# Causal attention and a two-stage mixer on one core: first loads four rows to a partition, scores in two jobs, a fourth Strassen pair and new ranks

## The chip, the core and the metric

The kernel runs on one core of a Trainium2 chip. The metric is the device time of one execution in microseconds; lower is better. The kernel before takes 565.9 us (median of 3 runs, 565.84 to 566.09).

## What is computed

```python
# q, k, v: (4, 12, 448, 64); seq 448, d_model 12 * 64 = 768
scores = scale * np.matmul(q, k.transpose(0, 1, 3, 2))
scores = np.where(np.triu(ones, k=1), -1e9, scores)          # causal
attn = np.exp(scores - scores.max(-1, keepdims=True))
attn = attn / (attn.sum(-1, keepdims=True) + 1e-09)
x = heads side by side of np.matmul(attn, v)                 # (4, 448, 768)
# the mixer; weights arrive as float64
h = np.maximum(x.T @ w_tok1, 0.0) @ w_tok2                   # 448 -> 256 -> 448, per batch
u = x + h.T
h2 = np.maximum(u @ w_ch1, 0.0) @ w_ch2                      # 768 -> 1536 -> 768
out = u + h2
```

## The kernel before, in words

**Jobs and a planner.** The kernel doesn't write its instructions in program order. It makes jobs (`Plan.job`), each with the engines that may do it and a cost in nanoseconds for each, the jobs that it needs, the buffers and PSUM banks that it holds, and a rank. `Plan.emit` then plays a clock of its own over those costs: whenever an engine is free it gives it the ready job of lowest rank, and writes that job's instructions. The order of instructions on each engine is therefore fixed when the program is built; on the chip each engine works through its own list in order and waits on semaphores. The costs and the ranks decide the order and nothing else.

**Fillers.** Up to 75 us on the planner's clock, TensorE (PE) is given matmuls of no use (`keep_warm`, L602, 128x512 bf16 on the mask) whenever it has no ready job and has been busy for less than a share `KEEP` of the time just past. They stand in PE's list like any other matmul.

**Attention.** The 48 heads are 24 pairs, in order of batch. `load_pair` fetches a pair's keys and queries (SP's queue; the queries of pair 0 on ACT's) in four DMAs each (L635), cut so that every partition gets 14 runs of 32 numbers, and `prep` turns them with one VectorE (DVE) 32x32 block transpose each (L667). `heads` makes the causal scores in 14 matmuls (L695) on four 64x64 corners of PE, fourteen blocks of 64 queries, into four PSUM banks; DVE adds the mask and takes the row minimum of the negated scores (L712), ScalarE (ACT) takes the exponential with its sum (L724), GpSimd (POOL) or another engine adds the guard (L743), DVE takes the reciprocal (L746), and the blocks are normalised (L343 on ACT, L345 on POOL or DVE). The probabilities are turned on PE (`flip`, L781) for pairs 0 to 11 and by DMA transpose for the others. `values` (L882) multiplies with v on 128x64 halves of PE, and `xturn` (L928) turns the result for the token stage.

**Mixer.** All products are in float32 split into a high and a low part, three matmuls for one. `tokens` (L974, L1007) runs three times per batch. `channels` (L1056) runs by `STAGES`: an entry (quarter of the 12 hidden blocks, batches) does `NF` = 3 hidden blocks (18 matmuls each and batch), then six output tiles with 9 matmuls each and batch, each added to `u` by DVE (L1124). For batches 2 and 3 some hidden blocks are done instead by `group`: a pair of hidden blocks times two batches is a 2x2 product of blocks, and Strassen's form needs 7 products of 9 matmuls (L1376) instead of 8. The output side of a group (L1444) has 6 matmuls per tile, and one DVE add. `combined` makes the sums of the weights, `mixtures` those of the inputs; before, `mixtures` runs late, rebuilds batch 2's input from its two parts (`again`) and keeps the sums in buffers that attention has left.

```python
STAGES = ((0, (0,)), (1, (0, 1)), (2, (0, 1)), (3, (0, 1)), (0, (1, 2)), (3, (2, 3)), (0, (3,)))
GROUPS = ((3, 4), (5, 6), (7, 8))
```

The last stage ends in `finish`, which adds, turns (L1472) and sends the last tile of the output.

Of the kernel before, what the change touches and what calls it, by code (L numbers as in the profile page):

```python
# [19 lines left out]

class Slot:


    def __init__(self, ring):
        self.ring = ring
        self.index = ring.uses
        self.left = 0
        self.tile = None
        ring.uses += 1

    def take(self):
        self.ring.taken.append(self)
# [16 lines left out]
class Bank:  # L49


    def __init__(self, plan, kind, share):
        self.plan, self.kind, self.share = plan, kind, share
        self.left = 0
        self.bank = None

# [4 lines left out]
    def take(self):  # L61
        p = self.plan
        self.bank = p.banks.pop(0)
        p.used[self.kind] = p.used.get(self.kind, 0) + 1
# [6 lines left out]
class Job:  # L71
    def __init__(self, order, costs, fn, rank, moved, lock=False):
        self.order, self.costs, self.fn, self.rank, self.moved, self.lock = order, costs, fn, rank, moved, lock
        self.waits = 0
        self.ready = 0.0
        self.after = []
        self.takes = []
        self.holds = []
# [4 lines left out]
class Plan:  # L83
# [7 lines left out]
    WINDOW, KEEP, WARM = 3400.0, 0.65, 75000.0  # L91
    LAG = {"pe": 230.0, "act": 150.0, "dve": 150.0, "pool": 150.0, "sp": 100.0}
    OWN = {"pe": 0.0, "act": 100.0, "dve": 130.0, "pool": 100.0, "sp": 100.0}
# [28 lines left out]
    def job(self, costs, fn, needs=(), holds=(), rank=0.0, moved=0.0, lock=False):  # L122

        j = Job(len(self.jobs), costs, fn, rank, moved, lock)
# [4 lines left out]
        for s in holds:  # L129
            if s.left == 0:  # L130
                j.takes.append(s)
            s.left += 1
# [4 lines left out]
    def emit(self):  # L137
        now = 0.0
        free = dict.fromkeys(self.ENGINES, 0.0)
        port = {"dve": 0.0, "pool": 0.0}  # L140
        dma = 0.0

        def until(j, e, t):
# [3 lines left out]
            return t + j.costs[e]  # L147
# [17 lines left out]
        while left:  # L165
# [3 lines left out]
            for e in self.ENGINES:  # L169
# [4 lines left out]
                while ready[e]:  # L174
# [4 lines left out]
                    open_ = all(s.open() for s in j.takes) and self.fits(j)  # L179
# [29 lines left out]
                end = until(pick, e, now)  # L209
                if e == "pool" or (e == "dve" and pick.lock):  # L210
                    port[e] = end
                free[e] = end
                if e == "pe":
                    self.spans.append((now, end))
                if pick.moved:
                    dma = end = max(end + 650.0, dma) + pick.moved
                    end += 800.0
                heapq.heappush(events, (end, 0, pick.order, pick))
# [25 lines left out]
def kernel(  # L244
# [72 lines left out]
    def act_ps(n):  # L317
        return 160.0 + 0.833 * n

    def act_sb(n):  # L320
        return 200.0 + 0.833 * n

    def dve1(n):
        return 150.0 + 1.04 * n
# [1232 lines left out]
```

## Time and profile before

| | |
|---|---|
| median of 3 runs | 565.9 us (565.84 to 566.09) |
| the profiled execution | 566.33 us, its span 564.6 us |
| busy PE / DVE / ACT / POOL | 548.2 / 395.0 / 304.7 / 223.1 us |
| PE matmul records | 3512, of them 55 fillers |

The page gives the engines' busy times; the windows give the same by stretch; the chain of waits follows the work that ended last back through what released it; the timeline lists an engine's instructions with the idle time ahead of each in brackets. A busy PE in the windows and the page is one with a matmul in flight. A float32 matmul on a part of the array has two records.

### The profile page before, as it was taken

Reading aid. Unit: us, or ns where it says so; the run is one execution under the profiler, and the core shown is the slowest. Engines: PE = TensorE matmul, PEld = TensorE weight load, DVE = VectorE, ACT = ScalarE, POOL = GpSimd, SP = SyncE. Lnnn points to the kernel's source line nnn. Section 1 sums busy time; section 2 is a strip of 40 time slices with the busy share of each in tenths; the row PEclk is TensorE's granted clock in tenths of the full one; section 3 lists DMA queues with packets and bytes.
Section 4 is the critical chain, followed back from the end, with each engine's and each line's share of the span. In section 5 each row is a group of like instructions: output and inputs, shape, how many; then the busy total and the mean of one; then the engine's idle time right before and its main releaser. Section 6 shows DMA issues by size and latency. Waiting matters only on the chain.

```text
span 564.6 us, 10295 instructions
## 1 busy us (share of the span) xinstructions
PE 548.2 (97%) x3512; PEld 473.5 (84%) x3512; DVE 395.0 (70%) x925; ACT 304.7 (54%) x746; POOL 223.1 (40%) x320
## 2 busy tenths in 40 slices
PE   8789999999999999999999999999999999999996
PEld 4467888878888988988988988988999998999995
DVE  4575868588777677778867687566576668677835
ACT  3678888787687566776667754674143120111010
POOL 2465675535352321430353621353356546232001
PEclk9999999999999999999999999999999999999999
DMA  6777647576988689789996766766221030312525
GB/s 112 157 154 149 155 104 174 161 180 150 197 224 190 149 203 204 177 222 200 217 217 132 151 111 122 148 126 127 62 74 56 29 111 2 111 55 86 126 57 99
DMA packets 230340, 77.37 MB, mean 137 GB/s; under 512 B 206544, under 2 KB 219024, under 8 KB 230288
## 3 DMA queue, kind: packets, MB, share of 16 engines
q1 hardware_dynamic: 217056, 74.99, 58.6%
q10 hardware_dynamic: 13232, 1.72, 1.8%
q8 instruction: 28, 0.46, 0.3%
q14 instruction: 24, 0.20, 0.1%
HBM read 49.15 MB, written 14.94 MB: 114 GB/s over the span
## 4 chain that ended last, share of the span: by engine, by line
PE 90%; SPq 3%; ACT 3%; DMA 2%; DVE 1%; issue 0%; POOL 0%; DVEq 0%; ACTq 0%
PE ps L1056 48%; PE ps L1444 8%; PE ps L882 7%; PE ps L1376 6%; PE ps L1007 5%; PE ps L974 5%; PE ps L695 5%; PE ps L781 3%; SPq L635 2%; PE ps L928 2%; DMA wl<-in_moe_w_tok_dram 1%; ACT prob L724 1%; SPq L400 1%; ACT pt L343 0%; DMA kq<-in_q_dram 0%
## 5 line engine op out<-in xcount | busy, mean ns | idle before, releaser
L1124 DVE TENSOR_TENSOR u<-ps,u 128x448 f32<-128x448 f32 x107 | 66.3, 622 | 47.1 <-PE ps L1056 33.6
L724 ACT ACTIVATE prob<-prob,stat 128x448 f32<-128x448 f32 (+6 forms) x168 | 84.0, 504 | 26.1 <-DVE stat L712 25.9
L345 POOL TENSOR_SCALAR prob<-prob,stat 128x448 f32<-128x448 f32 (+6 forms) x125 | 69.9, 572 | 39.7 <-DVE stat L746 36.7
L1056 PE MATMUL ps<-gh,wh 128*128 128x448 f32 x216 | 80.6, 373 | 0.0
L1056 PE MATMUL ps<-gh,wl 128*128 128x448 f32 x216 | 79.0, 366 | 0.0
L1056 PE MATMUL ps<-gl,wh 128*128 128x448 f32 x216 | 79.0, 366 | 0.0
L1056 PE MATMUL ps<-uh,wh 128*128 128x448 f32 x198 | 75.0, 379 | 0.0
L1056 PE MATMUL ps<-uh,wl 128*128 128x448 f32 x198 | 72.5, 366 | 0.0
L1056 PE MATMUL ps<-ul,wh 128*128 128x448 f32 x198 | 72.4, 366 | 0.0
L345 POOL TENSOR_SCALAR wh<-wf 128x768 fp32r<-128x768 f32 x27 | 23.1, 854 | 113.4 <-PE ps L1056 65.1
L712 DVE CUSTOM_DVE_ANT_0 prob<-ps,mask 128x448 f32<-128x448 f32 (+6 forms) x168 | 62.3, 412 | 0.3 <-PE ps L695 0.3
L743 POOL TENSOR_SCALAR stat<-stat 128x3 f32<-128x3 f32 (+1 forms) x43 | 13.3, 309 | 96.5 <-ACT prob L724 95.0
L882 PE MATMUL ps<-pt,vraw 128*64 128x448 f32 (+3 forms) x384 | 46.8, 386 | 1.4 <-ACT pt L343 1.4
L882 PEld LDWEIGHTS ps<-pt,vraw 128*64 128x64 f32 x384 | 25.4, 136 | 25.0 <-issue 14.0
L349 ACT COPY pt<-pt 128x512 uint16<-128x512 uint16 (+1 forms) x46 | 36.8, 875 | 15.5 <-DMA pt<-prob 15.4
L1056 PEld LDWEIGHTS ps<-gh,wh 128*128 128x128 f32 x216 | 40.6, 188 | 3.7
L1056 PEld LDWEIGHTS ps<-gl,wh 128*128 128x128 f32 x216 | 40.6, 188 | 3.5 <-DVE gl L1092 0.3
L1056 PEld LDWEIGHTS ps<-gh,wl 128*128 128x128 f32 x216 | 40.5, 188 | 3.2
L695 PEld LDWEIGHTS ps<-kq,kq 64*64 64x64 f32 x672 | 36.0, 132 | 8.3 <-issue 4.2
L695 PE MATMUL ps<-kq,kq 64*64 64x448 f32 (+6 forms) x672 | 41.8, 383 | 0.0
L354 DVE TENSOR_TENSOR wl<-wf,wh 128x768 fp32r<-128x768 f32 x35 | 35.9, 1033 | 8.5 <-ACT wh L343 4.9
L1056 PEld LDWEIGHTS ps<-uh,wh 128*128 128x128 f32 x198 | 37.2, 188 | 3.7
(144 smaller groups left out, 1224.2 us busy)
## 6 DMA issues: line engine op xcount, KB each, us to landing
wraw<-in_moe_w_ch_dram SPq DMA_DIRECT2D x24, 768.0 KB, 5.3
wf<-scratch SPq DMA_DIRECT2D x30, 384.0 KB, 3.2
scratch<-wf SPq DMA_DIRECT2D x24, 384.0 KB, 5.8
vraw<-in_v_dram SPq DMA_DIRECT2D x48, 96.0 KB, 2.4
out_dram<-kq SPq DMA_DIRECT2D x68, 56.0 KB, 1.8
kq<-in_k_dram SPq DMA_DIRECT2D x60, 56.0 KB, 3.9
kq<-in_q_dram SPq DMA_DIRECT2D x56, 56.0 KB, 2.5
gh<-in_k_dram SPq DMA_DIRECT2D x36, 56.0 KB, 2.3
```

What stands on the lines that cost most here:

```text
L345: eng[e].tensor_scalar(dst, src, scale, 0.0, op0=ALU.mult, op1=ALU.add)
L349: nc.scalar.copy(out, in_)
L354: eng[e].tensor_tensor(dst, a, b, op=ALU.subtract)
L695: nc.tensor.matmul(scores[r].tile[lanes, WHERE[c]:WHERE[c] + wide(c)], lhsT=qe.tile[LANES[j], c * QC:(c + 1) * QC], rhs=ke.tile[LANES[j], ...
L712: nc.vector.tensor_tensor_reduce(out=part(c, r), in0=ps.tile[:, WHERE[c]:WHERE[c] + wide(c)], in1=mask[:, S - wide(c):], scale=-SCALE, sca ...
L724: nc.scalar.activation(part(c, r), part(c, r), AF.Exp, bias=stat.tile[:, 0, AT[c]:AT[c] + 1], scale=-1.0, accum_out=stat.tile[:, 1, AT[c]: ...
L882: nc.tensor.matmul(ps.tile[LANES[j], c * QC:(c + nq) * QC], lhsT=s.tile[:, kb, j], rhs=view[:, o:o + nq, j], start=(kb == 0), stop=(n == 3),)
L974: nc.tensor.matmul(ps.tile[:, :PART], lhsT=w[:, c, m * P:(m + 1) * P], rhs=x.tile[:, c, :], start=(n == 0), stop=(n == len(work) - 1),)
L1056: nc.tensor.matmul(ps.tile[:, :S], lhsT=x.tile[:, at_:at_ + P], rhs=y, start=(n == 0 and i == 0), stop=(n + 1 == w[2] and i == 2),)
L1124: eng[e].tensor_tensor(u, ps.tile[:, :S], u, op=ALU.add)
L1376: nc.tensor.matmul(ps.tile[:, :S], lhsT=l()[:, t * P:(t + 1) * P], rhs=r, start=(t == 0 and n == 0), stop=(t == half - 1 and n == 2),)
L1444: nc.tensor.matmul(ps.tile[:, :S], lhsT=l.tile[:, t * P:(t + 1) * P], rhs=r.tile, start=(n == 0), stop=(n == 3 * len(fs) - 1),)
```

## The change

It does six things:

1. The keys and queries of pairs 0 and 1 are loaded with four neighbouring rows to a partition (112 partitions, two DMAs each instead of four; runs of 256 bytes in the tile instead of 128) into the buffers `uh` and `ul`, turned by four PE transposes each (`turn_runs`, L768 after the change) and copied back from PSUM by ACT or DVE. DVE's block transposes of these four tensors go.
2. The scores of a pair are two jobs: rounds 0 and 1, then rounds 2 and 3, each with its own two PSUM banks. The order of the 14 matmuls alternates between the two heads.
3. Hidden blocks 9 to 11 of batches 2 and 3 leave `channels` and become a group of one block (11), which is plain, and a fourth Strassen pair (9, 10).
4. `mixtures` is written right after attention, takes the inputs from `u` before anything is added to it (`again` goes), keeps some sums in the token weights' buffers, and adds to `u` wait for it.
5. `store` turns its tiles into the buffers `h1h` and `h1l`.
6. The planner has other costs, lags, and models of the DMA rings and of PE's change between tile shapes; KEEP is 0.7; a table `NUDGE` of some 110 numbers moves ranks of single jobs.

```diff
+NUDGE = {
+    "load_pair.load": {2.5: -0.3, 4.5: 1, 6.5: 4, 32.5: -38, 44.5: 24},
...
-    WINDOW, KEEP, WARM = 3400.0, 0.65, 75000.0
+    WINDOW, KEEP, WARM = 3400.0, 0.7, 75000.0
...
-    STAGES = ((0, (0,)), (1, (0, 1)), (2, (0, 1)), (3, (0, 1)), (0, (1, 2)), (3, (2, 3)), (0, (3,)))
+    STAGES = ((0, (0,)), (1, (0, 1)), (2, (0, 1)), (3, (0, 1)), (0, (1, 2)), (0, (3,)))
...
-    GROUPS = ((3, 4), (5, 6), (7, 8))
+    GROUPS = ((11,), (9, 10), (3, 4), (5, 6), (7, 8))
...
+            def whole(e, s=s, src=src):
+                make(s, [RUNS, RUN, 2, D], F32)
+                for j in range(2):
+                    eng[e].dma_start(
+                        out=s.tile[:, :, j], in_=src[b, 2 * t + j].rearrange("(p c) d -> p c d", c=RUN)
+                    )
...
+    def turn_runs(s, x, js, rank):
+
+        ps = share("t")
+
+        def turn(e):
+            bank(ps)
+            for c in range(RUN):
+                nc.tensor.transpose(
+                    ps.tile[:, c * RUNS:(c + 1) * RUNS], flat(s.tile[:, c]), ident[:RUNS, :RUNS]
+                )
+
+        def back(e):
+            copy(
+                e, make(x, [P, S], F32).rearrange("p (t c) -> p t c", c=RUN),
+                ps.tile[:, :S].rearrange("p (c t) -> p t c", c=RUN),
+            )
+
+        a = plan.job({"pe": pe(0, 0, 0, 0)}, turn, js, [s, ps], rank, turn=True)
+        return plan.job({"act": act_ps(S), "dve": dve1(S)}, back, [a], [ps, x], WRANK)
...
-        m = plan.job({"pe": 1900.0}, qk, ready + [last_qk[0]], holds, rank)
-        last_qk[0] = m
+        for rg, cost in zip(RG, (930.0, 740.0)):
+            holds = [x for r in rg for x in (scores[r], probs[r])] + [ke, qe, stat]
+            m = plan.job({"pe": cost}, lambda e, rg=rg: qk(e, rg), ready + [last_qk[0]], holds, rank, tiled=True)
...
-            x1, j1, f1 = mix("T1", t, p1, at(u3, t), ALU.subtract, [i1] + n3, [e1, u3])
+            x1, j1, f1 = mix("T1", t, at(u2, t), at(u3, t), ALU.subtract, [n2, n3], [u2, u3])
...
-    for stage in range(len(STAGES) - 2):
+    mixtures()
+    for stage in range(len(STAGES) - 1):
         channels(stage)
-    mixtures()
-    channels(len(STAGES) - 2)
-    for number in range(len(GROUPS)):
-        group(number, 6.0 + number * 0.63)
+    at = FIRST_GROUP
+    for number, fs in enumerate(GROUPS):
+        group(number, at)
+        at += SPAN[len(fs) - 1]
```

SP's list at its head, before (kq, gh, gl hold a pair's raw keys or queries, vraw its values; x4 is four DMAs):

```order
L635 DMA kq_106<-in_k_dram 32x14x32 x4
L635 DMA gh_126<-in_k_dram 32x14x32 x4
L635 DMA gl_134<-in_q_dram 32x14x32 x4
L644 DMA vraw_98<-in_v_dram 128x3x64 x2
L648 DMA vraw_98<-in_v_dram 64x2x64
L635 DMA gh_176<-in_k_dram 32x14x32 x4
L635 DMA gl_186<-in_q_dram 32x14x32 x4
L644 DMA vraw_100<-in_v_dram 128x3x64 x2
L648 DMA vraw_100<-in_v_dram 64x2x64
```

The same place of SP's list now:

```order
L707 DMA uh_109<-in_k_dram 112x4x64 x2
L707 DMA uh_117<-in_k_dram 112x4x64 x2
L707 DMA ul_126<-in_q_dram 112x4x64 x2
L724 DMA vraw_98<-in_v_dram 128x3x64 x2
L728 DMA vraw_98<-in_v_dram 64x2x64
L724 DMA vraw_100<-in_v_dram 128x3x64 x2
L728 DMA vraw_100<-in_v_dram 64x2x64
L715 DMA gh_172<-in_k_dram 32x14x32 x4
L715 DMA gl_198<-in_q_dram 32x14x32 x4
```

Six issues are gone ahead of pair 1's queries' end, and the values of pair 1 have moved ahead of pair 2's keys and queries.

DVE's list at its head, before (the four transposes are pairs 0 and 1; the ISA rows are L712 of pair 0 with the read of its minimum):

```order
L596 MEMSET zero 128x64
L667 STREAM_TRANSPOSE kq_142<-kq_106 128x448
L667 STREAM_TRANSPOSE kq_150<-kq_111 128x448
L667 STREAM_TRANSPOSE kq_174<-gh_126 128x448
L667 STREAM_TRANSPOSE kq_181<-gl_134 128x448
L712 ISA prob_0_90,stat_184<-ps_156,mask 128x448
L712 ISA stat_184 128x1
L712 ISA prob_0_91,stat_184<-ps_157,mask 128x384
```

DVE's list at its head now:

```order
L665 MEMSET zero 128x64
L826 ISA prob_0_90,stat_187<-ps_162,mask 128x448
L826 ISA stat_187 128x1
L826 ISA prob_0_91,stat_187<-ps_163,mask 128x384
L826 ISA stat_187 128x1
L826 ISA prob_0_91,stat_187<-ps_163,mask 128x128
```

No transpose stands ahead of pair 0's masking any more. Further down, pair 0's reciprocal stood behind the transpose of pair 2's keys and now stands ahead of it.

PE's list at the scores of pair 2, before (L695; `ps` are PSUM banks; the first six of 14):

```order
L695 MATMUL ps_309<-kq_216,kq_247 64x448
L695 MATMUL ps_310<-kq_216,kq_247 64x384
L695 MATMUL ps_311<-kq_216,kq_247 64x320
L695 MATMUL ps_312<-kq_216,kq_247 64x256
L695 MATMUL ps_310<-kq_216,kq_247 64x128
L695 MATMUL ps_312<-kq_216,kq_247 64x192
```

The same place of PE's list now (L806 scores, L895 turning of probabilities, L671 a filler):

```order
L806 MATMUL ps_295<-kq_240,kq_270 64x448 x2
L806 MATMUL ps_296<-kq_240,kq_270 64x384 x2
L806 MATMUL ps_296<-kq_240,kq_270 64x128 x2
L895 MATMUL ps_305<-ident,prob_0_93 128x128 x4
L671 LDWEIGHTS mask
L671 MATMUL ps_89<-mask 128x512
L806 MATMUL ps_322<-kq_240,kq_270 64x256 x2
L806 MATMUL ps_321<-kq_240,kq_270 64x320 x2
```

Before, the 14 matmuls of a pair always stood together; now other work stands between the halves of some pairs.

## Rows read from the trace of the kernel before

**Rows 1.** The page, busy us, share of the span, instructions:
```profile
PE 548.2 (97%) x3512; PEld 473.5 (84%) x3512; DVE 395.0 (70%) x925; ACT 304.7 (54%) x746; POOL 223.1 (40%) x320
```

**Rows 2.** Windows: stretch, its length, each engine's busy us, PE's granted clock, DMA share:
```profile
0.00:20.00 20.00, 15.65 (x116) 8.81 (x120) 8.77 (x37) 8.90 (x25) 7.07 (x29) 1.00 0.69 137
20.00:45.00 25.00, 19.74 (x189) 14.24 (x182) 17.23 (x60) 18.29 (x61) 14.04 (x29) 1.00 0.74 142
45.00:65.00 20.00, 20.00 (x182) 15.72 (x183) 14.55 (x59) 18.12 (x62) 13.02 (x25) 1.00 0.71 146
65.00:160.00 95.00, 93.96 (x751) 80.19 (x750) 70.94 (x196) 76.31 (x214) 48.54 (x77) 1.00 0.69 168
160.00:440.00 280.00, 280.00 (x1706) 246.20 (x1705) 201.09 (x451) 167.30 (x364) 102.73 (x132) 1.00 0.69 152
440.00:520.00 80.00, 78.61 (x388) 72.36 (x387) 55.25 (x82) 10.67 (x17) 33.21 (x28) 1.00 0.21 65
```

**Rows 3.** Chain of waits, in order of time: start us, us, what:
```profile
22.45 2.23 DMA gl<-in_q_dram
...
44.97 1.95 PE ps L882 x16
...
51.73 1.08 PE ps L602 x5
...
58.26 0.44 PE ps L928 x4
```

**Rows 4.** Timeline of PE, start: start us, us, engine, line, operation [idle before <-releaser]:
```profile
1.40 5.75 PE L602 MATMUL ps<-mask 128*128 128x512 bf16 x17 [1.40 <-POOL mask L364]
7.08 1.74 PE L695 MATMUL ps<-kq,kq 64*64 64x448 f32 x28
8.76 2.76 PE L602 MATMUL ps<-mask 128*128 128x512 bf16 x12
...
62.83 0.38 PE L974 MATMUL ps<-xh,w1hi 128*128 128x256 f32 x1
```

**Rows 5.** Timeline of PE's weight loads: two of the first fillers' loads:
```profile
4.78 0.15 PEld L602 LDWEIGHTS <-mask 128*128 128x128 bf16 x1 [0.28 <-issue]
5.21 1.45 PEld L602 LDWEIGHTS <-mask 128*128 128x128 bf16 x7 [0.28 <-issue]
```

**Rows 6.** Timeline of DVE, pairs 0 to 2:
```profile
5.10 1.17 DVE L667 STREAM_TRANSPOSE kq<-kq 128x448 f32<-128x448 f32 x2 [4.18 <-DMA kq<-in_k_dram]
...
9.07 0.65 DVE L667 STREAM_TRANSPOSE kq<-gl 128x448 f32<-128x448 f32 x1 [1.77 <-DMA gl<-in_q_dram]
9.64 0.59 DVE L712 CUSTOM_DVE_ANT_0 prob<-ps,mask 128x448 f32<-128x448 f32 x1
...
13.10 0.65 DVE L667 STREAM_TRANSPOSE kq<-gh 128x448 f32<-128x448 f32 x1 [1.00 <-DMA gh<-in_k_dram]
```

**Rows 7.** Timeline of ACT: the first exponential of pair 0:
```profile
10.28 0.67 ACT L724 ACTIVATE prob<-prob,stat 128x448 f32<-128x448 f32 x1 [6.20 <-DVE stat L712]
```

**Rows 8.** Timeline of SP's queue, DMA issues:
```profile
5.07 2.05 SPq L635 DMA_DIRECT2D gl<-in_q_dram  x4
```

**Rows 9.** DMA issues of the page: times, KB each, us to landing:
```profile
vraw<-in_v_dram SPq DMA_DIRECT2D x48, 96.0 KB, 2.4
```

**Rows 10.** Chain of waits, two stretches of PE alone:
```profile
439.81 13.41 PE ps L1056 x66
453.21 10.96 PE ps L1376 x54
```

**Rows 11.** Timeline of PE around one pair's scores:
```profile
58.97 0.38 PE L602 MATMUL ps<-mask 128*128 128x512 bf16 x1
59.27 1.74 PE L695 MATMUL ps<-kq,kq 64*64 64x448 f32 x28
```

**Rows 12.** The page's groups: DVE's adds to u:
```profile
L1124 DVE TENSOR_TENSOR u<-ps,u 128x448 f32<-128x448 f32 x107 | 66.3, 622 | 47.1 <-PE ps L1056 33.6
```

**Rows 13.** Timeline of PE: the first output of the first Strassen pair that waits:
```profile
467.57 0.47 PE L1444 MATMUL ps<-gl,wh 128*128 128x448 f32 x1 [1.39 <-DVE gl L1312]
```

More of the change, by code (lines that the diff above doesn't have):

```diff
@@ L18 @@
 PSUM = bass.MemoryType.PSUM
+NUDGE = {
+    "token_weights.<lambda>": {3.5: -11},
+    "xturn.<lambda>": {-1: -18, 37: 12},
+    "load_pair.load": {2.5: -0.3, 4.5: 1, 6.5: 4, 32.5: -38, 44.5: 24},
+    "heads.low": {2: 10, 6: 1},
+    "xturn.twice": {1: 9, 9: 6, 13: 11},
+    "load_pair.blocks": {2: 0.3, 6: -1, 10: -12, 12: -8, 36: -4, 38: 28, 40: 27},
+    "by_tensor.evac": {4: -3},
+    "values.pv": {4: 2, 12: 6, 24: -12},
+    "values.evac": {4: 24},
+    "heads.recip": {6: 3, 20: 5, 44: 1},
+    "tokens.tok1": {8.5: -32, 32.5: -5},
+    "by_tensor.flip": {8: -3.2, 18: 2},
+    "split_u.hi": {12.5: -1.5},
+    "prep.turn": {10.5: -7, 42.5: -5},
+    "heads.expo": {12: -1.1, 18: 6, 22: 0.1, 24: 0.04, 38: 42, 42: -2},
+    "xturn.lo": {11: 24, 19: 10, 33: 6, 37: 12},
+    "by_tensor.norm": {14: -4, 16: 14},
+    "heads.guard": {16: 12, 42: 34},
+    "heads.<lambda>": {20: -2, 34: -13, 42: -31, 44: -24, 46: 18},
+    "tokens.tok2": {24.5: -3, 28.5: 4},
+    "by_dma.split": {26: -2, 40: 15},
+    "xturn.turn": {31: 5},
+    "by_dma.turn": {34: -3, 42: 18},
+    "by_dma.norm": {42: -0.2},
+    "channel_weights.<lambda>": {12: -10, 19: -6},
+    "channels.up": {28.667: 4, 29.333: 10, 39.667: 7, 40.167: 5, 40.833: 14, 45.333: 14, 47.333: 16},
+    "channels.down": {30: -18, 30.5: -5, 37.75: -22, 38.5: 17, 44: -13, 54.25: 5, 55: 31.6, 55.5: 31.3, 77.09: -32},
+    "add.plus": {-6: 16},
+    "narrow.load": {16: -5, 23: -15, 26: -6, 33: -3},
+    "narrow.join": {17: 16},
+    "narrow.size": {30: 21},
+    "group.up": {57.34: 3, 57.68: 6},
+    "hidden.lo": {-6: 7},
+    "group.down": {60.23: 4, 69.75: 1.6},
+    "group.product.do": {59.85: 6, 60.39: 10, 60.66: 7, 63.36: -11, 66.87: 4, 67.68: 9, 68.22: 35},
+    "combined.split.lo": {-4.93: 10},
+    "parts.<lambda>": {-4.93: 2},
+}
 class Slot:
@@ L131, in job @@
                 j.takes.append(s)
+            elif s not in j.takes:
+                j.joins.append(s)
             s.left += 1
@@ L178, in emit @@
                         continue
-                    open_ = all(s.open() for s in j.takes) and self.fits(j)
+                    open_ = all(s.got for s in j.joins) and all(s.open() for s in j.takes) and self.fits(j)
                     if open_ and len(j.costs) > 1:
@@ L383, with narrow @@
     CRANK, CSTEP, CLEAD, WLEAD, TRANK = 2.0 * H - 6.0, 6.0, -9.0, 6.0, 3.5
-    def narrow(n, shape, source, f, rank, needs=(), raw=None):
+    def narrow(n, shape, source, f, rank, needs=(), raw=None, issues=1):
         raw = raw or slot("wraw")
@@ L415, in join @@
             )
-        j = plan.job({"sp": 520.0}, load, holds=[raw], rank=rank, moved=move(shape[0] * n * 8))
-        j = plan.job({"act": act_sb(n)}, size, [j, *needs], [raw, f], rank)
+        moved, ring = (3000.0, 60) if n > 2 * P else (800.0, 16)
+        j = plan.job({"sp": 530.0 * issues}, load, holds=[raw], rank=rank, moved=moved, ring=ring)
+        j = plan.job({"act": 115.0 + 0.92 * n}, size, [j, *needs], [raw, f], rank)
         j = plan.job({"dve": dve2(n)}, shift, [j], [f], rank, lock=True)
@@ L1135, in add @@
         begun[b, t] = times + 1, last
-        if times + 1 == (NQT if b < 2 else 2 + len(GROUPS)):
+        if times + 1 == (NQT if b < 2 else sum(b in bs for _, bs in STAGES) + len(GROUPS)):
             store(b, t, last)
```

208 lines of the change are left out of this document (124 added, 84 removed).

## The prediction

> **What bounds the kernel now.** I began with the busy times. PE has a matmul in flight for 97% of the span, DVE for 70%, ACT 54%, POOL 40% [rows 1]. So PE is the bound, and the question for each edit is whether it takes work off PE's list or shortens a stretch in which PE has nothing to do. The windows say where such stretches are [rows 2]: PE lacks 4.35 us of the first 20 and 5.26 of the next 25, nothing from 45 to 65 us, 1.04 us from 65 to 160, nothing from 160 to 440, and 1.39 us from 440 to 520. About 9.6 us of waits lie ahead of 45 us. The timeline of PE shows that its busy time there isn't all work either: 17 fillers ahead of the first scores at 7.08 us, 12 more ahead of the second [rows 4], 55 up to 59 us by PE's list. One costs 0.215 us (five take 1.08 [rows 3]), at the start 0.43 (their weight loads follow each other by 5.21 - 4.78 [rows 5]). So the first 60 us hold some 21 us that no result needs (55 x 0.215 + 9.6), and from there to 520 us waits take less than 3.
>
> Who holds up the start? The chain of waits runs through SP's issues and a load of pair 3's queries at 22.45 us, and from 44.97 on through PE alone, fillers among it [rows 3]. DVE shows two waits at loads which stand ahead of pair 0's work in its list: 1.77 us for pair 1's queries, with pair 0's masking behind it, and 1.00 for pair 2's keys, with pair 0's reciprocal behind that [rows 6]. ACT is near its limit only from 45 to 65 us (18.12 of 20 [rows 2]).
>
> **Term 1, the fourth Strassen pair.** Two hidden blocks of two batches took 8 blocks of 9 matmuls on the input side and now take 7; the output side keeps its count. PE loses 9 matmuls. 66 of them take 13.41 us, 54 of the Strassen kind 10.96 [rows 10], both 0.203 us each: -1.83 us, on a PE that never waits from 160 to 440 us. It brings 12 more adds to `u` of 0.622 us on DVE [rows 12], 7.5 us. DVE has 79 us spare from 160 to 440 and 25 from 440 to 520 [rows 2], so I cost them at nothing; if that cover fails they come out as a wait at a group's end, which is a rival below. The early input sums take off six additions of POOL's and put the others where DVE has room; nothing, by the same rows.
>
> **Term 2, scores in two jobs.** The scores' own columns don't change. What changes is how often PE goes between full tiles, 64x64 corners and 128x64 halves: by the lists 87 times before, 101 now, 18 and 29 of them ahead of the second token stage. A filler that should take 0.215 us is followed by scores after 0.30 [rows 11]: one change costs 0.09 us. Behind the second token stage it is three more changes: +0.3 us. Ahead of it eleven: +1.0, counted in term 3. The alternating order of the 14 matmuls could gain or lose something inside a pair. A pair takes 1.68 us from its first matmul to the next filler [rows 4]; I take nothing, with 0.05 us a pair, 1.2 in all, either way.
>
> **Term 3, the start.** The second token stage, which begins at 62.83 us [rows 4], is a good mark: the lists ahead of it hold the same seven pairs' scores, twenty turnings and five pairs' values. Ahead of it stood 55 fillers and now stand 34: 21 x 0.215 = -4.5 us. The new 16 transposes are four jobs like the four L928 transposes of 0.44 us [rows 3]: +1.8. With the changes of shape, +1.0, PE's own list is 1.7 us shorter up to the mark. The rest is its waits, 9.6 us.
>
> How do these go? The first load is two DMAs of 112 KB in 256-byte runs; the nearest row is the values, 96 KB in such runs, 2.4 us to landing [rows 9], so I expect pair 0's queries and keys some 4 us after the start, where DVE had them at 5.10 [rows 6]. But six fillers, three, and four now stand ahead of and between the turnings, and the scores of pair 0 stand behind pair 1's first turning as well, then wait for two copies on ACT. I put them at 7 to 8 us, no earlier than the 7.08 of before. Behind that the gain comes. Pair 0's masking no longer stands behind the load of pair 1's queries, so it can start with the first half of the scores; its reciprocal no longer stands behind pair 2's keys. These were waits of 1.77 and 1.00 us. And SP issues six DMAs fewer, each about 0.51 us (four in 2.05 [rows 8]), so pair 3's load is 3.1 us earlier. Against this, half scores leave PE with more to wait for, and fewer fillers hide waits. The bounds on the waits' change are -6 us (most of them go) and +1.7 (they grow by as much as PE's list shrinks). I take -1.8, the size of the first DVE wait, since that one loses its cause: term 3 is -1.7 - 1.8 = -3.5 us.
>
> The granted clock is 1.00 in every window [rows 2]. [...] With the change PE stops after the sixth filler, at about 1.40 + 6 x 0.43 = 4 us, and waits for a load. [...]
>
> **Term 4, late waits.** There are three groups before and five now. One of the three ended in a wait of PE, 1.39 us, for DVE's low part of the hidden block [rows 13]: the products were done at 453.21 + 10.96 = 464.17 [rows 10], the outputs ran on from 467.57. In the new list two of the four Strassen pairs have two products of the next one between their last product and their first output, 3.6 us of cover; two have none, as two had none before. I take 0, bounds -1.4 and +6.
>
> **Sum.** -1.83 + 0.3 - 3.5 + 0 = -5.0 us. The profiled execution took 566.33 us, 1.7 more than its span; the sum gives 561.3 there. The median of the runs is 0.4 lower, so the forecast is **560.9 us**. A measurement of this kernel tells about 0.2%, 1.1 us, from no change.
>
> **Rivals.**
> - *The start opens up.* If the waits ahead of 45 us fall from 9.6 to 4 and the wait at the group's end goes, the gain is 5.6 - 1.8 = 3.8 and 1.4 more: 555.7 us. For it speaks that loads and DVE held PE up, and both are relieved; against it that ACT has only 2 us spare between 45 and 65 us [rows 2], and that 34 fillers remain.
> [...]
> - *The change doesn't do what it says:* no gain at the start, and term 1 lost in adds that PE waits for, which leaves the +0.3: 566.2 us.
> - *Slower: a wait at each group's end.* The hidden block of a pair's last product passes DVE, ACT and DVE before the outputs can start, and DVE now has 12 more adds and the adds of short output tiles (three matmuls, 0.61 us, against an add of 0.622 [rows 12]) in its list. If DVE is behind, each of the five groups ends in a wait of 1.4 us or more; at the whole chain from 464.17 to 467.57, 3.4 us, it is 5 x 3.4 - 1.4 = 15.6 more. From 1.3 us each on (5 x 1.3 - 1.4 = 5.1) the gain is eaten; I price it at 2 us each, +8.6: 569.5 us. For it speaks the row of before [rows 13]; against it that DVE had 31% spare there [rows 2] and that two ends have cover.
>
> **How the numbers follow.** The forecast, 558 to 562.5, gets 0.47. The open start gets 0.20, the start that gives nothing 0.18 (two thirds of it below 564.8), no effect 0.04, slower 0.11. That makes faster by over 0.2% 0.47 + 0.20 + 0.12 = 0.79, within 0.2% 0.06 + 0.04 = 0.10, slower 0.11. The range leaves out the slower case, 0.11, and the lower part of the open start, 0.08: 555 to 566.5 us.
>
> **What would show it.** Right: pair 0's first exponential before 9.5 us, where it was at 10.28 [rows 7], although its scores don't come earlier; the waits of DVE at loads ahead of pair 0's work gone; the second token stage at about 59.3 us; no PE wait between 160 us and the first group. Wrong: a second token stage at 57 us or less (open start) or at 62 or more (nothing); PE idle of over 1 us at several group ends; a granted clock under 1.00 in the first 20 us.

## The result and the profile after

The changed kernel takes **561.26 us** (median of 4 runs, 559.97 to 562.56) against 566.0 for the kernel before on the same chip: a ratio of 0.9913, 95% interval 0.9890 to 0.9935. Run again later beside the last experiments it took 561.2 us (6 runs, 560.39 to 563.13), ratio 0.9921 (0.9903 to 0.9939). The gain is 4.7 us by the medians and 4.5 to 4.9 by the ratios; forecast were 5.0.

The profiled execution was the fastest of its four, 559.97 us with a span of 558.2. That of the second measurement took 562.06 us, span 560.2. What is read from one of them alone is therefore checked against the other.

Busy time on the page after, and its group of adds to `u` (for [rows 1] and [rows 12]):

```profile
PE 548.1 (98%) x3500; PEld 465.0 (83%) x3500; DVE 400.6 (72%) x939; ACT 316.7 (57%) x794; POOL 193.9 (35%) x280
L1241 DVE TENSOR_TENSOR u<-ps,u 128x448 f32<-128x448 f32 x119 | 72.7, 618 | 40.6 <-PE ps L1173 21.7
```

The list of PE is what the prediction counted: 12 records fewer (9 fewer Strassen matmuls, 19 fewer fillers in all, 16 turnings more), and 12 more adds. Windows after, columns as in [rows 2]:

```profile
0.00:20.00 20.00, 16.44 (x125) 9.32 (x129) 7.04 (x36) 11.12 (x33) 6.35 (x27) 1.00 0.69 153
20.00:45.00 25.00, 24.95 (x221) 18.10 (x222) 21.31 (x79) 24.62 (x83) 17.47 (x36) 1.00 0.73 137
45.00:65.00 20.00, 19.78 (x176) 14.32 (x176) 13.12 (x48) 18.30 (x62) 10.77 (x24) 1.00 0.62 129
65.00:160.00 95.00, 95.00 (x758) 77.37 (x753) 73.89 (x214) 80.50 (x230) 49.18 (x71) 1.00 0.76 170
440.00:520.00 80.00, 79.45 (x387) 72.22 (x386) 58.13 (x88) 12.55 (x20) 26.40 (x21) 1.00 0.21 65
```

Against [rows 2], PE's waits ahead of 45 us fell from 9.6 us to 3.6 (3.56 + 0.05). ACT, the fourth engine of a row, was busy for 18.29 of the 25 us from 20 to 45 and is now busy for 24.62 of them (22.79 in the second execution). PE's 24.95 there hold fillers; that they cover waits, so that PE isn't the bound there, is what no_late_fill below shows.

The start on the timeline of PE after, and the second token stage (for [rows 4]):

```profile
1.40 2.74 PE L671 MATMUL ps<-mask 128*128 128x512 bf16 x6 [1.40 <-POOL mask L430]
5.33 0.98 PE L768 MATMUL ps<-ident,ul 112*128 112x112 f32 x4 [1.20 <-DMA ul<-in_q_dram]
6.10 1.49 PE L671 MATMUL ps<-mask 128*128 128x512 bf16 x3
7.38 0.95 PE L768 MATMUL ps<-ident,uh 112*128 112x112 f32 x4
8.13 1.43 PE L671 MATMUL ps<-mask 128*128 128x512 bf16 x4
9.40 0.55 PE L768 MATMUL ps<-ident,uh 112*128 112x112 f32 x4
9.88 1.75 PE L806 MATMUL ps<-kq,kq 64*64 64x448 f32 x28
...
56.17 0.39 PE L1090 MATMUL ps<-xh,w1hi 128*128 128x256 f32 x1
```

The first scores come at 9.88 us (before 7.08), so 2.8 us later, and still the second token stage begins 6.7 us earlier than at 62.83. ACT's first exponential, for [rows 7], is later as well:

```profile
11.68 0.67 ACT L838 ACTIVATE prob<-prob,stat 128x448 f32<-128x448 f32 x1 [1.16 <-DVE stat L826]
```

The gain lies behind it, in what ACT waits for. ACT's waits from 10 to 57 us, before (engine, line, what it waited for, total us, times, longest us):

```profile
ACT prob L724 <- DVE stat L712: 7.0, 2, 6.2
ACT wf L403 <- DMA wl<-in_moe_w_tok_dram: 3.9, 2, 2.5
ACT prob L343 <- DVE stat L746: 1.9, 1, 1.9
ACT pt L343 <- PE ps L781: 1.5, 3, 1.0
ACT u L343 <- PE ps L882: 0.9, 2, 0.7
ACT xh L343 <- PE ps L928: 0.7, 1, 0.7
```

The same after, from 14 us on:

```profile
ACT xl L409 <- DVE xl L420: 1.0, 1, 1.0
ACT pt L409 <- PE ps L895: 0.4, 2, 0.2
ACT xh L409 <- PE ps L1042: 0.2, 1, 0.2
```

Without the first exponential's own wait of 6.2 us, 9.7 us of waits became 1.6 (2.8 in the second execution).

Where the time went, by three marks: the second token stage, the last product of the mixer on PE (the last matmul of L1056 before, of L1173 after), the end of the span. The last row is a kernel of the experiments, "best". The last product before:

```profile
559.17 0.37 PE L1056 MATMUL ps<-gh,wl 128*128 128x448 f32 x1
```

And after:

```profile
551.72 0.36 PE L1173 MATMUL ps<-gh,wl 128*128 128x448 f32 x1
```

| profiled execution | stage begins | stage to last product | last product to end | span |
|---|---|---|---|---|
| before | 62.83 | 496.34 | 5.38 | 564.55 |
| after | 56.17 (-6.66) | 495.55 (-0.79) | 6.45 (+1.07) | 558.17 (-6.38) |
| after, again | 57.74 (-5.09) | 495.91 (-0.43) | 6.53 (+1.15) | 560.18 (-4.37) |
| best | 56.23 | 496.01 | 5.33 | 557.57 |

So the start gains 5.1 to 6.7 us, the long middle 0.4 to 0.8, and the tail, of which the prediction didn't speak, gives back 1.1. Behind the stage the changed kernel is 0.3 to 0.7 us slower than before: the whole gain lies in the start. The 1.6 us between the two executions of one kernel lie in the start as well: in the second ACT waits 1.4 us for a load of token weights that it doesn't wait for in the first. Two kernels of the experiments that keep the order up to this mark have it at 56.16 (tail_kq) and 57.77 us (three_pairs), so one trace gives the mark to some 1.6 us.

### The profile page after: what moved, and what is told of

The parts are those of the page before. It is cut to its first block, busy times and chain, and to the rows that moved or that the text cites. A ratio compares the mean times of both kernels' runs of the same rounds, so it can differ in the third digit from the quotient of the medians.

```text
span 558.2 us, 10296 instructions
## 1 busy us (share of the span) xinstructions
PE 548.1 (98%) x3500; PEld 465.0 (83%) x3500; DVE 400.6 (72%) x939; ACT 316.7 (57%) x794; POOL 193.9 (35%) x280
## 4 chain that ended last, share of the span: by engine, by line
PE 67%; DVE 1%; issue 0%; DMA 0%; ACT 0%; ACTq 0%; DVEq 0%
PE ps L1173 34%; PE ps L1554 12%; PE ps L1486 8%; PE ps L996 3%; PE ps L1090 3%; PE ps L1123 3%; PE ps L806 2%; PE ps L1463 1%; PE ps L1042 1%; DVE wl L420 0%; DMA out_dram<-h1h 0%; DVE gl L1422 0%; DVE kq L1516 0%; ACTq L1608 0%; DVE h1h L1604 0%
## 5 line engine op out<-in xcount | busy, mean ns | idle before, releaser
L1173 PE MATMUL ps<-gh,wh 128*128 128x448 f32 x180 | 67.0, 372 | 0.0
L1173 PE MATMUL ps<-gl,wh 128*128 128x448 f32 x180 | 66.0, 367 | 0.0
L1173 PE MATMUL ps<-gh,wl 128*128 128x448 f32 x180 | 65.9, 366 | 0.0
L1173 PE MATMUL ps<-uh,wh 128*128 128x448 f32 x162 | 60.7, 375 | 0.0
L1173 PE MATMUL ps<-uh,wl 128*128 128x448 f32 x162 | 59.3, 366 | 0.0
L1173 PE MATMUL ps<-ul,wh 128*128 128x448 f32 x162 | 59.3, 366 | 0.0
L806 PE MATMUL ps<-kq,kq 64*64 64x256 f32 (+6 forms) x672 | 45.1, 386 | 0.1
L1417 ACT ACTIVATE gh<-kq 128x448 fp32r<-128x448 f32 x16 | 8.9, 576 | 59.4 <-DVE kq L1516 59.4
L806 PEld LDWEIGHTS ps<-kq,kq 64*64 64x64 f32 x672 | 27.8, 132 | 17.4 <-issue 10.0
L1554 PE MATMUL ps<-gh,wh 128*128 128x448 f32 x108 | 39.6, 367 | 0.4 <-ACT gh L1417 0.4
L1554 PE MATMUL ps<-gl,wh 128*128 128x448 f32 x108 | 39.8, 368 | 0.1
L1554 PE MATMUL ps<-gh,wl 128*128 128x448 f32 x108 | 39.5, 366 | 0.0
L1173 PEld LDWEIGHTS ps<-gl,wh 128*128 128x128 f32 x180 | 33.9, 188 | 2.9 <-DVE gl L1209 0.2
L1173 PEld LDWEIGHTS ps<-gh,wh 128*128 128x128 f32 x180 | 33.8, 188 | 3.0
```

The costliest lines, as they stand in the source:

```text
L806: nc.tensor.matmul(scores[r].tile[lanes, WHERE[c]:WHERE[c] + wide(c)], lhsT=qe.tile[LANES[j], c * QC:(c + 1) * QC], rhs=ke.tile[LANES[j], ...
L1173: nc.tensor.matmul(ps.tile[:, :S], lhsT=x.tile[:, at_:at_ + P], rhs=y, start=(n == 0 and i == 0), stop=(n + 1 == w[2] and i == 2),)
L1554: nc.tensor.matmul(ps.tile[:, :S], lhsT=l.tile[:, t * P:(t + 1) * P], rhs=r.tile, start=(n == 0), stop=(n == 3 * len(fs) - 1),)
```

## Experiments

Eleven other kernels were run, and the changed kernel again, each timed beside the kernel before on the same chip.

### At the start: fillers

**head_fill** puts ten fillers instead of six ahead of the first turning.

```diff
+        self.fills = 0
...
-                        self.filler.fn(e)
+                        self.fills += 1
+                        for _ in range(5 if self.fills == 6 else 1):
+                            self.filler.fn(e)
```

> The changed kernel with ten fillers instead of six ahead of the first turning; all other instructions keep their order. In the changed kernel PE breaks off at 4 us, waits until 5.3 us for pair 0's queries, and its fillers keep the low pitch of 0.43 us until about 9 us. Theory (the clock rose late because of that break, and the start still counts, since PE and ACT hardly wait behind it): the low pitch ends at about 5.3 us, pair 0's scores start at about 8.3 us instead of 9.88, the second token stage at about 54.8 instead of 56.2, and the time is 1.3 to 1.6 us shorter. Rival (the waits at 13 to 16 us swallow it): the scores start earlier, the token stage and the end do not, under 0.4 us.

Measured: 559.97 us (559.58 to 560.68), ratio 0.9897 (0.9883 to 0.9911). Timeline of PE at its start:

```profile
1.40 4.04 PE L674 MATMUL ps<-mask 128*128 128x512 bf16 x10 [1.40 <-POOL mask L433]
5.28 0.55 PE L771 MATMUL ps<-ident,ul 112*128 112x112 f32 x4
5.66 0.81 PE L674 MATMUL ps<-mask 128*128 128x512 bf16 x3
6.31 0.55 PE L771 MATMUL ps<-ident,uh 112*128 112x112 f32 x4
6.70 1.03 PE L674 MATMUL ps<-mask 128*128 128x512 bf16 x4
7.56 0.55 PE L771 MATMUL ps<-ident,uh 112*128 112x112 f32 x4
8.04 1.75 PE L809 MATMUL ps<-kq,kq 64*64 64x448 f32 x28
```

In this execution the first four turnings take 0.55 us, not 0.95. (Whether the missing break is the reason isn't shown; two other traces, in the last section, speak against it.) The first scores come 1.8 us earlier, but the second token stage at 56.31 us is no earlier than 56.17. Of the 1.8 us the scores of pair 2 keep 1.0 (17.05 us against 18.06), behind a new PE wait of 0.76 us for DVE, and by 50 us nothing is left. The medians differ by 1.2 to 1.3 us, but the intervals of the two kernels overlap. By the traces PE's lateness at the start costs nothing up to the stage, which fits ACT being the bound behind it.

**no_late_fill** takes the last 20 fillers away.

```diff
+        self.fills = 0
...
-                        self.filler.fn(e)
+                        self.fills += 1
+                        for _ in range(0 if self.fills > 16 else 1):
+                            self.filler.fn(e)
```

> The changed kernel without its last 20 fillers (all behind pair 1's scores); all other instructions keep their order. PE has next to no waits from 20 to 45 us, so one theory is that these fillers stand in the way: 20 x 0.215 = 4.3 us shorter, or a good part of that. The theory that I hold: ACT is the bound there (24.6 of 25 us busy), the fillers lie in PE's waits for it, and they come back as waits: 0 to 0.8 us shorter. Third: PE's granted clock falls in the first 60 us without them, and it gets slower.

Measured: 560.5 us (560.31 to 561.4), ratio 0.9909 (0.9896 to 0.9921), the stage at 56.1 us. Twenty fillers by 0.215 are 4.3 us of PE's list, and PE's idle time up to 520 us grows from 4.4 to 8.4 us; the granted clock is 1.00 in every window up to there. What a filler covers comes back as a wait. A shorter list of fillers is no gain of itself, and term 3 had counted 4.5 us of it as one.

### The loads

**old_loads** takes back part 1 alone (all pairs loaded in four DMAs and turned by DVE); the planner then makes a new order.

```diff
-    EARLY = 2
+    EARLY = 0
```

> The changed kernel with the loads and block transposes of before for pairs 0 and 1; the planner orders anew. Theory A (the early loads bring the early gain, through six issues fewer on SP's queue): 2 to 4 us slower, about 564. Theory B (the gain of the start comes from the planner's new costs and ranks, which remove the waits of pairs 1 to 4; the new loads bring no earlier first exponential, 11.68 against 10.28 us, and four copies more on a busy ACT): within 1.5 us of the changed kernel, and DVE waits again at pair 1's load.

Measured: 573.16 us (568.69 to 574.34), ratio 1.0119 (1.0090 to 1.0148), slower than before. But the stage begins at 61.0 us, still ahead of 62.83; the loss lies behind it, in a PE wait of 2.4 us for `xl`, four waits from 308 to 331 us, and 3.4 us of slow work behind the first of them (granted clock 0.50 from 64 to 66 us; a matmul of the token stage takes 0.415 us there, 0.283 in head_fill). Those are faults of the new order, so this run doesn't price the loads. The next one does.

**old_loads_frozen** keeps the order of the planner that the changed kernel has and changes only what the jobs of pairs 0 and 1 write.

```diff
-                make(s, [RUNS, RUN, 2, D], F32)
-                for j in range(2):
+                make(s, [P, S // 32, 32], F32)
+                for n in range(4):
+                    j, o = divmod(n, 2)
                     eng[e].dma_start(
-                        out=s.tile[:, :, j], in_=src[b, 2 * t + j].rearrange("(p c) d -> p c d", c=RUN)
+                        out=s.tile[32 * n:32 * n + 32],
+                        in_=src[b, 2 * t + j, :, 32 * o:32 * o + 32].rearrange("(c i) d -> i c d", i=32),
                     )
...
-            bank(ps)
-            for c in range(RUN):
-                nc.tensor.transpose(
-                    ps.tile[:, c * RUNS:(c + 1) * RUNS], flat(s.tile[:, c]), ident[:RUNS, :RUNS]
-                )
+            pass
...
-            copy(
-                e, make(x, [P, S], F32).rearrange("p (t c) -> p t c", c=RUN),
-                ps.tile[:, :S].rearrange("p (c t) -> p t c", c=RUN),
-            )
+            nc.vector.transpose(make(x, [P, S], F32), s.tile.rearrange("p c d -> p (c d)"))
```

> The changed kernel with the planner's decisions kept as they are, but with the old form of the four early loads at their places: four DMAs each, a block transpose on DVE where the copy back stood, nothing on PE. (In old_loads the planner ordered everything anew, so that run couldn't tell the loads from the order.) ACT is without waits from 14 to 57 us in the changed kernel and would have four copies less, about 2.1 us; SP issues six DMAs more, 3.1 us. Theory (ACT sets the pace at the start; loads are a small part): within 1.5 us of the changed kernel, second token stage at 55 to 58 us. Rival (the loads bring the early gain): second token stage at 59 us or later, 2 to 4 us slower than the changed kernel.

Measured: 562.07 us (561.48 to 563.59), ratio 0.993 (0.9918 to 0.9943), by the medians 0.8 to 0.9 us above the changed kernel, within what the intervals can tell. The first scores come at 6.5 us, 3.4 earlier, the second token stage at 59.12, later by 1.4 to 3.0, but still 3.7 ahead of the kernel before. So the time is the theory's and the stage the rival's. DVE's transposes are back ahead of the masking, and PE waits behind ACT. Its waits:

```profile
PE ps L890 <- ACT prob L409: 3.6, 2, 2.6
```

**before_new_loads** is the kernel before with part 1 alone, under the old planner.

```diff
+    EARLY = 2
+    RUN = 4
+    RUNS = S // RUN
...
+            early = g < EARLY and nm != "v"
+            if early:
+                s = slot({"k": "uh", "q": "ul"}[nm])
...
+            if g < EARLY:
+                ready.append(turn_runs(s, x, js, rank))
+                continue
...
```

> The kernel before with part 1 of the change alone: new loads and PE turnings for pairs 0 and 1, the planner of before. Theory (the early gain is the order's, not the loads'): within 1.5 us of the kernel before, second token stage at 61 us or later. Rival (the loads' six fewer issues on SP bring it): 2 to 4 us faster, second token stage at 60 us or earlier.

Measured: 567.23 us (566.52 to 570.06), ratio 1.0022 (1.0013 to 1.0031): a little slower. In its trace (of its slowest execution, 570.06 us) the first scores are at 7.91 us, the stage at 63.24. The loads by themselves bring nothing; with the order of the changed kernel they bring under 1 us by the medians, and 1.4 to 3.0 at the second token stage in single traces.

### The order

**no_nudge** empties the table of ranks; the costs, lags and models of the planner stay.

```diff
-NUDGE = {
-    "token_weights.<lambda>": {3.5: -11},
...
-}
+NUDGE = {}
```

> The changed kernel with an empty table of nudges. Its PE list has the same products, and 43 fillers instead of 36. Theory (the order is worth as much as the parts; old_loads lost 12 us by a new order under nudges that no longer fit): 3 to 8 us slower than the changed kernel, with new waits of PE behind 65 us or a later second token stage. Rival (the costs do it, the nudges are trimmings): within 1.5 us.

Measured: 569.7 us (567.81 to 572.53), ratio 1.0065 (1.0040 to 1.0089): 8 us slower than the changed kernel, and slower than before. The stage begins at 58.22 us, so most of the start's gain is there without the table. The loss lies in the middle. Timeline of PE, the longest wait from 335 to 360 us:

```profile
354.76 3.44 PE L958 MATMUL ps<-pt,vraw 128*64 128x448 f32 x16 [3.44 <-ACT pt L377]
```

After the wait of 3.44 us the 16 products with v take 3.44 us too, where they take 1.95 elsewhere; the granted clock is 0.54 from 354.76 to 358.10 us. This long wait is paid for again, by 1.5 us, in what follows it.

**one_job** makes the scores of a pair one job again; the planner makes a new order.

```diff
-        for rg, cost in zip(RG, (930.0, 740.0)):
+        for rg, cost in (((0, 1, 2, 3), 1670.0),):
```

> The scores of a pair are one job of four banks again, and the planner makes a new order from the same ranks: 72 fillers stand in it instead of 34. Theory (two jobs let the masking and the exponentials start earlier and leave PE other work between the halves; 10 pairs really split, at 0.25 us each, are the price): the second token stage at 59 us or later instead of 56.2, total 563 to 568 us. Rival (the halves only cost, and PE's list is shorter without them): 558.7 us, 10 x 0.25 below the changed kernel.

Measured: 589.8 us (588.13 to 592.38), ratio 1.0428 (1.0400 to 1.0455): worse than either theory had. The stage begins at 64.64 us, behind 67 fillers instead of 34 (33 x 0.215 = 7.1 us). PE is idle for 23.7 us of the first 583 by its trace, 18.2 of them behind 390 us. The longest:

```profile
405.17 3.68 PE L996 MATMUL ps<-pt,vraw 128*64 128x448 f32 x16 [6.78 <-DVE pt L417]
```

PE stands 6.78 us for DVE's copies of turned probabilities and the 16 products behind that take 3.68 us (granted clock 0.52 from 405.2 to 409.0 us), much as in no_nudge. This says again that an order for which the ranks weren't set is bad by 8 to 29 us. It doesn't give the worth of the halves: that would take one job under an order made for it, which wasn't tried.

**Which part feeds ACT.** ACT's busy time up to 45 us (its windows 0 to 20 and 20 to 45) sorts these kernels, though it also counts the copies that the new order gives to ACT (316.7 us in all against 304.7):

| kernel | ACT busy to 45 us | PE idle to 45 us | second token stage |
|---|---|---|---|
| before | 27.2 | 9.6 | 62.83 |
| before_new_loads (old planner) | 29.2 | 9.8 | 63.24 |
| old_loads | 35.1 | 4.5 | 60.95 |
| old_loads_frozen | 32.6 | 6.9 | 59.12 |
| no_nudge | 35.7 | 4.0 | 58.22 |
| one_job | 35.3 | 2.9 | 64.64 |
| after / again | 35.7 / 34.1 | 3.6 / 4.3 | 56.17 / 57.74 |

Everything planned with the new costs, lags and models keeps ACT busy, whether or not it has the table, the halves or the new loads; frozen under the wrong loads it is still nearer to after. The old planner does not, with either kind of loads. That most of the early gain comes with the new order is shown: with the loads of before the stage begins 3.7 us earlier under it, with the new loads 5.1 to 6.7, and under the old planner the new loads gain nothing. That within the order it is the costs and models, is argued by elimination: the kernel before with the new costs alone wasn't run, and parts 4 and 5 of the change are in all the new kernels too. How the costs share the stage's 5.1 to 6.7 us with the halves isn't settled either, since one_job keeps ACT just as busy and then spends its time on fillers.

### The fourth Strassen pair

**three_pairs** puts blocks 9 to 11 back into `channels`.

```diff
-    STAGES = (..., (0, (1, 2)), (0, (3,)))
+    STAGES = (..., (0, (1, 2)), (3, (2, 3)), (0, (3,)))
...
-    FIRST_GROUP = 5.0
+    FIRST_GROUP = 5.0 + 0.34 + 0.63
...
-    GROUPS = ((11,), (9, 10), (3, 4), (5, 6), (7, 8))
+    GROUPS = ((3, 4), (5, 6), (7, 8))
```

> The changed kernel with blocks 9 to 11 of batches 2 and 3 back in the plain stages: three Strassen pairs, 1701 matmuls in the channel part instead of 1692. The first half of the program keeps its order. Theory (a PE that hardly waits pays each matmul): 9 x 0.203 = 1.8 us slower than the changed kernel. Rival (12 adds fewer on DVE and one group end fewer give it back): same within 0.5 us, or faster.

Measured: 562.14 us (561.62 to 563.92), ratio 0.9932 (0.9920 to 0.9945): 0.9 us above the changed kernel's median, an amount that the intervals don't part from 0 or from 1.8. Its trace says more: from the second token stage (57.77) to the last product (554.22) it takes 496.45 us, 0.5 to 0.9 more than the two executions of after, and more than any of the kernels that keep the order there (495.0 to 496.0). It has no wait of PE from 440 to 520 us; the changed kernel has one at 514 us, of which the timeline of PE shows

```profile
514.74 0.44 PE L1554 MATMUL ps<-gh,wh 128*128 128x448 f32 x1 [0.42 <-ACT gh L1417]
```

and, with the output before it, starts come 0.95 us later than their pitch. So nine matmuls are saved, 1.83 us, and about half comes back as this one wait at a group's end. What stands against the 1.83 is seen in traces, not in the medians. The traced execution, 563.92 us, is also the slowest of the six, and its tail is longer than after's, 7.85 us against 6.45, since its last turning on DVE waits 1.86 us for the buffer `h1h`; so not all of the 0.9 us between the medians need be matmuls.

### The tail

**tail_order** turns batch 3's last tiles into the two buffers of `kq` again and lets the tile that is done in two parts end the list, as before.

```diff
-    "channels.down": {..., 55.5: 31.3, 77.09: -32},
+    "channels.down": {..., 55.5: 31.3},
...
-        o = slot(("h1h", "h1l")[t % 2])
+        o = slot("kq" if b == B - 1 else ("h1h", "h1l")[t % 2])
```

> The changed kernel, with batch 3's stores back in the kq buffers and the nudge of the last output tile taken out, so that the tile that is sent in two parts is the last on PE again; nothing ahead of the last two tiles moves. In the changed kernel 5.9 us lie between the last matmul and the end, before 4.1: the last tile's add, a wait for the buffer, a block transpose and four DMA issues of ACT. Theory: the end is 1.5 to 1.8 us earlier. Rival: the last DMAs are held up by the earlier stores on the two queues, and the end moves by less than 0.5 us.

Measured: 559.15 us (558.98 to 560.06), ratio 0.9884 (0.9870 to 0.9899), 2.1 us below the changed kernel. **tail_kq** has the second edit alone.

> The last batch's output tiles are turned into the two-buffer ring of the raw keys again; the order is the changed kernel's, instruction for instruction. Theory: the buffers h1h and h1l, one each, are what lengthened the tail, from 4.03 to 5.87 us behind the last matmul, since the last turning waits 0.40 us for the store before it and stands behind it: -0.4 to -0.9 us, 560.4 to 560.9. Rival: the order of the last two output tiles costs the rest and the buffer nothing: within 0.2 us of the changed kernel.

Measured: 560.24 us (559.81 to 561.1), ratio 0.9903 (0.9888 to 0.9919), against 561.2 for **after_again** in the same comparison; the two intervals overlap.

> The changed kernel unaltered, as the yardstick of the other three runs. Both theories: 560.5 to 561.8 us, ratio about 0.991.

The timeline of the end after, all engines:

```profile
551.92 0.60 PE L1582 MATMUL ps<-ident,u 128*112 128x128 f32 x4
...
552.12 0.62 DVE L1241 TENSOR_TENSOR u<-ps,u 128x448 f32<-128x448 f32 x1 [0.59 <-PE ps L1173]
...
553.15 0.65 DVE L1604 STREAM_TRANSPOSE h1h<-u 128x448 f32<-128x448 f32 x1 [0.40 <-DMA out_dram<-h1h]
...
553.83 1.96 ACTq L1608 DMA_DIRECT2D out_dram<-h1h  x4
```

The last thing is now a whole tile: its add, a wait of 0.40 us for the buffer that the store before it still reads, the transpose, and four issues that take 1.96 us. The end of "best", which has tail_order's edits:

```profile
552.24 0.36 PE L1176 MATMUL ps<-gh,wl 128*128 128x448 f32 x1
553.08 0.72 PE L1585 MATMUL ps<-ident,u 128*112 128x128 f32 x4 [0.48 <-DVE u L1579]
553.55 0.76 DVE L414 TENSOR_SCALAR kq<-ps 112x256 f32<-112x256 f32 x2 [0.23 <-PE ps L1585]
554.15 0.44 ACTq L1593 DMA_DIRECT2D out_dram<-kq  x1
554.33 0.32 SPq L1593 DMA_DIRECT2D out_dram<-kq  x1
```

There only two parts of a tile are left behind the last turning, with one issue each, on two queues. From the last product to the end: 6.45 us after, 6.09 in tail_kq, 5.33 in tail_order, 5.38 before. The buffers are 0.4 us of the 1.1 and the order 0.8. By the medians tail_order gains 2.1 us, twice that. Where the rest lies the traces don't show: from the stage to the last product the executions of after and of the kernels with the same order there take 495.0 to 496.0 us.

**best** is tail_order with head_fill.

```diff
+        self.fills = 0
...
-                        self.filler.fn(e)
+                        self.fills += 1
+                        for _ in range(5 if self.fills == 6 else 1):
+                            self.filler.fn(e)
...
-    "channels.down": {..., 55.5: 31.3, 77.09: -32},
+    "channels.down": {..., 55.5: 31.3},
...
-        o = slot(("h1h", "h1l")[t % 2])
+        o = slot("kq" if b == B - 1 else ("h1h", "h1l")[t % 2])
```

> The two edits that were the fastest so far together: the raw keys' ring for the last stores with the last output tile in the old order, and ten fillers instead of six ahead of the first turning. Alone they took 559.15 and 559.97 us against 561.26. Theory (one works behind the last matmul, the other ahead of the first scores, and they add up): 558.0 to 558.9 us. Rival (what the fillers save at the start comes back as a wait for ACT within 25 us, so that only the tail's edit counts): 559.1 to 559.6.

Measured: **559.0 us** (558.71 to 559.36), ratio 0.9876 (0.9860 to 0.9893). It is the fastest kernel measured, 2.2 us under after_again in the same comparison, with the smallest spread. Against tail_order's 0.9884 (0.9870 to 0.9899) the difference can't be told; 559.0 lies between what the two readings gave. The tail's edits carry it.

## Why the prediction was right, point by point

- **The whole.** 560.9 us forecast, 561.26 and 561.2 measured. The number came out right by luck: the start gained 5.1 to 6.7 us where the sum had 3.5, the splits cost far more than term 2, and the tail costs 1.1 where the sum had nothing.
- **Term 1, -1.83 us.** The count of PE holds, and no trace shows a cost of the 12 adds on DVE, as said. Of the slower rival, a wait at each group's end, one wait of 0.95 us came true at one of five groups, far from the 1.3 each from which it would have decided. Term 4 put the late waits at 0; with the waits of [rows 13] and others shorter, PE's idle time from 65 to 520 us fell by 1.8 us, from 2.43 to 0.61 (by 1.3 in the second execution). From the stage to the last product the channel part of PE's list, counted from each start to the next, fell from 354.3 to 350.4 us: 1.84 for the nine matmuls, 0.6 for the shorter wait at a group's end, and 1.4 because fewer of its matmuls follow late.
- **Term 2, +0.3 us, mis-sized.** I priced only changes of shape, 0.09 us each. On the timeline of PE after, a pair that is really split:

```profile
45.34 1.09 PE L806 MATMUL ps<-kq,kq 64*64 64x448 f32 x12
46.36 0.66 PE L1042 MATMUL ps<-ident,u 128*128 128x128 f32 x4
...
49.85 0.97 PE L806 MATMUL ps<-kq,kq 64*64 64x256 f32 x16
50.76 0.66 PE L895 MATMUL ps<-across_ident,prob 128*128 128x128 f32 x4
```

  The halves hold PE for 46.36 - 45.34 = 1.02 and 50.76 - 49.85 = 0.91 us, 1.93 together, where an unsplit pair at 9.88 us holds it for 1.67 (11.55 - 9.88). That is 0.26 us a pair; averaged over the ten pairs that are split it is 0.25. Five stand behind the stage: +1.27 us, four times the term. The five ahead of it come to about what the +1.0 in term 3 had. And this isn't all: what isn't channel work between the stage and the last product (scores, turnings, values, token stages) rose from 142.1 to 145.1 us (145.5 in the second execution), 3.0 us or ten times the term.
- **Term 3, -3.5 us: the sign and the reason (waits) right, the size and the place wrong.** The step that failed is "I put them at 7 to 8 us" with "pair 0's first exponential before 9.5 us": they came at 9.88 and 11.68. The load landed at 5.3 us, not 4, and most of the seven fillers between the turnings followed each other by 0.43 us. The list came out as counted (34 fillers, turnings, shapes), but not as priced: from start to start the seven fillers took 2.55 us where 0.215 each gives 1.5, and the four turnings 2.44 where the term had 1.8. Against that, the waits ahead of 45 us fell by 6.0 us (5.3 in the second execution), not 1.8: the bound of -6 that I had as the best case. I had tied the waits to two loads in DVE's list [rows 6] and to six issues on SP. These brought 2.1 us on SP's queue, not 3.1: pair 1's queries are issued by 5.03 us (3.74 + 1.29), where it was 7.12 [rows 8], since a new issue takes 0.65 to 0.74 us. What fell was ACT's waiting, once its work had begun, and the runs above put that down to the order in the main. The forecast for the stage, 59.3 us, was missed by 1.6 to 3.1.
- **The rivals.** The start that gives nothing didn't come: the stage begins at 56.2 and 57.7 us, not at 62 or more. Fillers did follow each other by 0.43 us for longer, until about 9 us, but the first scores, at 9.88 us, took 1.67 us, like the 1.68 of before, and in head_fill, with its first scores 1.8 us earlier, the stage begins no earlier. A granted clock under 1.00 in the first 20 us couldn't have been the sign of it: the window from 5.33 to 9.00 us has 1.00, though the fillers in it follow each other by 0.43 us. "The start opens up" was closest in the waits, 9.6 to 4 as it says, with a stage under 57 us in one execution of two; its total was 5.5 us too low, of which the tail is 1.1 and the work between the channels 2.7 more than term 2.
- **What no term held: the tail, +1.1 us.** The change has part 5, the buffers `h1h` and `h1l`, and a table of ranks in which one number, -32, moves the last output tile. I costed neither. What stands behind the last matmul is covered by no other work of PE, so both needed a term of their own.
- **What stays open.** From the stage to the last product the two parts, -3.8 for the channels and +3.0 for the rest, make the -0.8 that was measured (-3.9 and +3.4 the -0.4 of the second execution). Of the +3.0 the halves of the scores are 1.27; how far the splits also cause the remaining 1.7, in the work that now stands between them, no run shows.

## What to carry to other kernels

Work behind the last matmul is read first: the tile that ends the list should be the one with the least left to add, turn and send, on two queues (5.33 us behind the last product in best, 6.45 after). Where an order is made from costs, an edit that lets it be made anew measures the order and not the edit (12 us against 0.8 for the same loads here), so freeze the order to price a part. Fillers and waits on the bound engine are one sum as long as another engine feeds it (4.3 us of fillers taken out here, 4.0 us of waits more): look for what that other engine waits for.

## What the runs showed of the hardware

- At the start fillers follow each other by 0.43 us, later by 0.215. The longer pitch lasted until about 9 us after, with a break from 4.1 us that ended with the load at 5.33, and until 5.2 us before, without a break. With ten fillers and no break (head_fill) the first turnings, at 5.28 us, took 0.55 us, as they do where the shorter pitch is. But a break doesn't decide it. In before_new_loads the same six fillers and a break of 1.20 us were followed by four turnings in 0.58 us:

```profile
5.33 0.58 PE L702 MATMUL ps<-ident,ul 112*128 112x112 f32 x4 [1.20 <-DMA ul<-in_q_dram]
```

  And in "best" ten fillers without a break were followed by four turnings in 0.95 us:

```profile
1.40 4.45 PE L674 MATMUL ps<-mask 128*128 128x512 bf16 x10 [1.40 <-POOL mask L433]
5.64 0.95 PE L771 MATMUL ps<-ident,ul 112*128 112x112 f32 x4
```

  So starts that look alike on PE up to the first turning had the shorter pitch by then in one kernel and not in another. The windows give 1.00 as the granted clock there (0.00 to 20.00 us: before, after, head_fill, before_new_loads), so it can't be read from them, and no run here shows what sets the pitch.
- After, the turnings went with the pitch beside them: four took 0.95 us at 7.38 us, behind fillers 0.43 us apart, and 0.55 at 9.40, where the weight loads of the last filler and the first turning are 0.22 us apart (8.97 and 9.19 us).
- A wait of 3.4 us in the middle (no_nudge) and one of 6.8 (one_job) were each followed by 16 products with v in 3.44 and 3.68 us, where they take 1.95, at a granted clock of 0.54 and 0.52; in one_job it was 0.50 in the last 3.1 us of the wait as well. Shorter waits were so followed in some places (2.4 us in old_loads, granted clock 0.50 from 64 to 66 us; 3.0 in one_job, matmuls 0.37 us apart instead of 0.20) and not in others (2.6 us in old_loads_frozen, granted clock 1.00 in every window up to 520 us).
- Splitting 14 matmuls on 64x64 corners into two groups costs 0.25 us, though the columns are the same (1.93 us for the two halves of one pair, 1.67 for a pair in one piece). What in the split takes that time no run here shows.
